# A token-mixing layer on one core: the fifth tile of x gets a load of its own

## Chip, core and metric

The kernel runs on one core of a Trainium2 chip. The metric is the time of one execution on the device in microseconds, and the median over several executions is compared. In the text, PE is the tensor engine, ACT the scalar engine, DVE the vector engine, POOL the general-purpose engine, and SP the engine that only issues transfers here.

## What is computed

The input `x` has 2048 tokens of 640 features in bf16. A linear attention with 32 heads of 20 features and a gated MLP mixer both work on it, and a gate of one number per token mixes the two.

```python
def _A_ref(x, wqkv, wo):
    qkv = (x @ wqkv).reshape(B, S, 3, H, Dh)        # S 2048, H 32, Dh 20; then per head
    phi = lambda t: jnp.where(t > 0, t + 1, jnp.exp(t)) + 1e-6
    pq, pk = phi(q), phi(k)
    kv = jnp.einsum("bhsd,bhse->bhde", pk, v)
    z = jnp.einsum("bhsd->bhd", pk)
    num = jnp.einsum("bhqd,bhde->bhqe", pq, kv)
    den = jnp.einsum("bhqd,bhd->bhq", pq, z)[..., None] + 1e-6
    return concat_heads(num / den) @ wo

def _B_ref(x, w1, w2, w3, w4):
    h = _gelu(_layernorm(x) @ w1)
    hs = shift_quarters(h) @ w2                     # quarters of h moved by 1, -1, 2, -2 tokens
    x1 = x + hs
    return x1 + _gelu(_layernorm(x1) @ w3) @ w4

g = _sigmoid((x * gate_w).sum(-1, keepdims=True))
return g * _A_ref(...) + (1 - g) * _B_ref(...)
```

## The kernel before

The tokens are cut into 16 tiles of 128. Each tile is held once as it comes (`x_tok`, tokens on the partitions) and once turned (`xT`, features on the partitions), because the projections need the features on the partitions. For each tile t the kernel computes q (`q_tile`, L864) and k (`k_tile`, L781): five matmuls of 512 columns and five of 128 or 130 each, then `phi` (L772): an Exp on ACT, and two operations on DVE that leave the result in bf16. In the text, q4 is the q matmuls of tile 4, k3 the k matmuls of tile 3, and so on.

The order in which PE does this is written out by hand at the start and planned afterwards. It begins with warm-up matmuls; tiles 0 to 2 are turned by PE itself; then q of tiles 0 to 2 (`q_three`), k of tiles 0 and 1 (`k_two`), k2, and from tile 3 on q and k in turn, q3, k3, q4, k4. From k4 on a short matmul for the gram matrix of x and k (`gt_tail`, L798) stands after each pair. After tile 15 come the rest of that gram matrix, the mixer's `w1` and `w2`, then `w3`, the attention output and `w4`.

A planner (`_Items`) models how long each step takes and picks the next one, and the tracker `_Sched` adds the semaphore waits that the data require. Each engine runs its own list of instructions in order.

Tiles 3 to 15 are turned by the DMA engines. `x_turn(t)` (L692) issues one transposing transfer on SP; it has to wait until the tile has landed in `x_tok`. SP's list at the start, in order, is:

1. the loads of tile 0, tile 1, the first 128-row slice of wq, tile 2, and the four other slices of wq
2. the first slice of the k weights (`wkg`), the load of tile 3, and the four other slices of `wkg`, the last at L688
3. the turn of tile 3 (L695), which waits for the load of tile 3
4. a load of tiles 4 to 7 in one transfer of 640 KB (L700), then the four turns of these tiles (L702)
5. the same for tiles 8 to 11 and for tiles 12 to 15

Every load above except those in 4 and 5 has 160 KB. As SP's list is in order, the load of tiles 4 to 7 is issued once the turn of tile 3 has been issued, and the load of tiles 8 to 11 once the turn of tile 7 has been issued.

POOL issues loads too, on a queue of its own, when certain k tiles are done: `load_w1` (L706) after k5, `load_w2` (L714) after k8, and `wv` and `wo` after k11. These share the 16 DMA engines with the turns of the later tiles.

Of the kernel before, what the change touches and what calls it, by code (L numbers as in the profile page):

```python
# [416 lines left out]
def _build(nc, A_x, A_wqkv, A_wo, B_w1, B_w2, B_w3, B_w4, gate_w, out, dbg=None, stop=None):  # L417
# [61 lines left out]
    x_tok = pa.alloc("x_tok", [128, NT, D], BF16)  # L479
# [191 lines left out]
    x2 = A_x[0]  # L671

    def dma_in(out_ap, in_ap, key, **kw):
        return sch.dma("sp", out_ap, in_ap, key, **kw)
# [17 lines left out]
    def x_turn(t):  # L692
        sch.dma("sp", xT[:, :, 128 * t:128 * (t + 1)], x_tok[:, t, :], "trx%d" % (t % 4), transpose=True)

    x_turn(3)  # L695
    gwr = xn[:, 1, 0:128]
    dve(lambda e: e.memset(gwr, 0.0), [], [gwr])
    sch.dma("act", xn[0:KD, 1, 0:128], gate_w.rearrange("(k p) -> k p", p=128), "gw")
    for c in range(1, NCH):
        dma_in(x_tok[:, 4 * c:4 * c + 4, :], x2[512 * c:512 * (c + 1), :].rearrange("(n p) d -> p n d", p=128), "xc%d" % c)  # L700
        for t in range(4 * c, 4 * c + 4):
            x_turn(t)  # L702

# [499 lines left out]
    for t in range(NT):  # L1203
        c = t // 4
# [53 lines left out]
    for t in range(NT):  # L1258
        c = t // 4
# [30 lines left out]
def bass_gated_mix__linear_attn_block__mixer_s_mlp__prompt_kernel(  # L1290
    nc, A_x, A_wqkv, A_wo, B_x, B_w1, B_w2, B_w3, B_w4, gate_w, out
):
    assert tuple(A_x.shape) == (1, S, D) and tuple(out.shape) == (1, S, D)
    assert tuple(A_wqkv.shape) == (D, 3 * D) and tuple(A_wo.shape) == (D, D)
    assert tuple(B_w1.shape) == (D, D) and tuple(B_w2.shape) == (D, D)
    assert tuple(B_w3.shape) == (D, F) and tuple(B_w4.shape) == (F, D) and tuple(gate_w.shape) == (D,)
    _build(nc, A_x, A_wqkv, A_wo, B_w1, B_w2, B_w3, B_w4, gate_w, out)
# [28 lines left out]
```

## Time and profile before

| what | us |
|---|---|
| median of 5 executions | 260.59 |
| the five | 260.57, 260.58, 260.59, 262.31, 262.43 |
| the profiled execution | 260.59 |
| its span in the trace | 259.3 |
| outside the span | 1.29 |
| PE busy in the span | 255.6 |
| granted PE clock, mean | 1.00 of full speed |

The span runs from the first to the last instruction in the trace. Matmuls are pipelined, and their ends are modelled: where two groups follow one another without a gap, the modelled end of the first lies after the start of the second. How long PE really stood is therefore read from the starts.

The three 640 KB loads of x, from issue to landing, took 4.4, 4.3 and 6.7 us. The 160 KB loads of x took 2.4 to 3.7 us, and the five of the k weights 3.8 to 4.0 us. The thirteen turns took between 2.4 and 8.7 us to land, 2.8 in the median, and each costs SP about 1.28 us to issue.

### The profile page before, as it was taken

Reading aid. Unit: us, or ns where it says so; the run is one execution under the profiler, and the core shown is the slowest. Engines: PE = TensorE matmul, PEld = TensorE weight load, DVE = VectorE, ACT = ScalarE, POOL = GpSimd, SP = SyncE. Lnnn points to the kernel's source line nnn. Section 1 sums busy time; section 2 is a strip of 40 time slices with the busy share of each in tenths; the row PEclk is TensorE's granted clock in tenths of the full one; section 3 lists DMA queues with packets and bytes.
Section 4 is the critical chain, followed back from the end, with each engine's and each line's share of the span. In section 5 each row is a group of like instructions: output and inputs, shape, how many; then the busy total and the mean of one; then the engine's idle time right before and its main releaser. Section 6 shows DMA issues by size and latency. Waiting matters only on the chain.

```text
span 259.3 us, 4291 instructions
## 1 busy us (share of the span) xinstructions
PE 255.6 (99%) x1685; PEld 131.9 (51%) x1685; DVE 152.6 (59%) x288; ACT 106.7 (41%) x216; POOL 93.7 (36%) x151
## 2 busy tenths in 40 slices
PE   7999999999999999999999999999999999999996
PEld 4555555544454554555444545554455644456453
DVE  2587887899913799999998407992033410143233
ACT  1496677751355766675854240005500045200000
POOL 4013995969954019667904202230011110021001
PEclk9999999999999999999999999999999999999999
DMA  6855989982856992552826650232000020000211
GB/s 183 237 139 151 131 222 158 201 133 50 99 110 125 346 344 42 67 101 52 104 47 122 124 74 0 44 87 73 0 3 0 3 101 0 0 3 1 104 51 51
DMA packets 51390, 25.16 MB, mean 97 GB/s; under 512 B 42750, under 2 KB 49959, under 8 KB 51370
## 3 DMA queue, kind: packets, MB, share of 16 engines
q1 hardware_dynamic: 49984, 21.47, 38.1%
q0 software_dynamic: 1136, 3.28, 5.4%
q8 instruction: 13, 0.21, 0.4%
q10 hardware_dynamic: 250, 0.14, 0.2%
q14 instruction: 7, 0.06, 0.1%
HBM read 12.05 MB, written 2.62 MB: 57 GB/s over the span
## 4 chain that ended last, share of the span: by engine, by line
PE 92%; DMA 4%; SPq 2%; DVE 0%; issue 0%
PE ps L600 60%; PE ps L1165 22%; PE ps L794 8%; DMA x_tok<-in_A_x_dram 3%; SPq L285 1%; DMA xT<-x_tok 1%; PE ps L1077 1%; PE ps L1147 1%; SPq L281 1%; DVE x_tok L639 0%; PE ps L967 0%; PE ps L996 0%; PE ps L1144 0%
## 5 line engine op out<-in xcount | busy, mean ns | idle before, releaser
L600 PE MATMUL ps<-xnT,w 128*128 128x512 bf16 x360 | 81.5, 379 | 0.0
L1165 PE MATMUL ps<-w,h2T 128*128 128x512 bf16 (+1 forms) x416 | 58.8, 299 | 0.0
L656 ACT ACTIVATE h2T<-ps 128x512 bf16<-128x512 f32 x52 | 30.5, 598 | 67.5 <-PE ps L600 67.5
L600 PEld LDWEIGHTS ps<-xnT,w 128*128 128x128 bf16 x360 | 34.2, 98 | 38.5 <-issue 0.9
L639 DVE SCALAR_TENSOR_TENSOR x_tok<-ps,stg,abx 128x512 bf16<-128x512 f32 (+1 forms) x32 | 17.3, 550 | 61.5 <-PE ps L1165 61.5
L622 POOL TENSOR_SCALAR abx<-x_tok,stg 128x640 f32<-128x640 bf16 x16 | 15.3, 959 | 98.9 <-DVE x_tok L639 94.9
L1165 PEld LDWEIGHTS ps<-w,h2T 128*128 128x128 bf16 x416 | 32.2, 98 | 24.9 <-issue 1.1
L622 POOL TENSOR_SCALAR xn<-x_tok,st 128x640 bf16<-128x640 bf16 x32 | 34.9, 1099 | 14.5 <-DMA xnT<-xn 13.9
L656 ACT ACTIVATE Er<-ps 128x640 bf16<-128x640 f32 x32 | 22.4, 707 | 17.1 <-PE ps L600 8.7
L655 ACT ACTIVATE junk<-x_tok 128x640 bf16<-128x640 bf16 x32 | 23.6, 739 | 3.1 <-DVE x_tok L637 2.6
L600 PE MATMUL ps<-M_sb,pqnT 128*128 128x512 bf16 (+1 forms) x160 | 24.3, 299 | 0.0
L656 ACT ACTIVATE hsT<-ps 128x512 bf16<-128x512 f32 (+1 forms) x32 | 18.9, 593 | 13.0 <-PE ps L600 12.7
L600 PE MATMUL ps<-w,hsT 128*128 128x512 bf16 (+1 forms) x160 | 23.7, 299 | 0.0
L639 DVE SCALAR_TENSOR_TENSOR abx<-ps,stg,abx 128x640 f32<-128x640 f32 x16 | 14.1, 884 | 12.4 <-PE ps L600 11.4
L600 PE MATMUL ps<-wkg,xT 128*128 128x130 bf16 (+1 forms) x140 | 21.4, 299 | 0.0
L600 PE MATMUL ps<-wq,xT 128*128 128x512 bf16 (+1 forms) x130 | 19.8, 299 | 0.2 <-DMA xT<-x_tok 0.2
L600 PEld LDWEIGHTS ps<-w,hsT 128*128 128x128 bf16 x160 | 13.3, 98 | 12.1
L600 PEld LDWEIGHTS ps<-M_sb,pqnT 128*128 128x128 bf16 x160 | 13.2, 98 | 10.9
L794 PE MATMUL ps<-pk_tok,x_tok 128*128 128x512 bf16 x80 | 17.8, 379 | 0.0
L622 DVE TENSOR_SCALAR Er<-Er 128x640 bf16<-128x640 bf16 x32 | 11.8, 369 | 9.7 <-ACT Er L656 9.6
L1106 DVE TENSOR_TENSOR pq_tok<-pq_tok,dnr 128x300 bf16<-128x300 bf16 (+1 forms) x48 | 16.9, 407 | 0.6
L637 DVE SCALAR_TENSOR_TENSOR x_tok<-ps,x_tok 128x640 bf16<-128x640 f32 x16 | 13.1, 821 | 6.4 <-PE ps L600 5.9
(78 smaller groups left out, 227.0 us busy)
## 6 DMA issues: line engine op xcount, KB each, us to landing
w<-in_B_w_dram SPq DMA_DIRECT2D x1, 2160.0 KB, 9.9
w<-in_B_w_dram SPq DMA_DIRECT2D x1, 2080.0 KB, 15.5
x_tok<-in_A_x_dram SPq DMA_DIRECT2D x3, 640.0 KB, 4.4
out_dram<-x_tok SPq DMA_DIRECT2D x3, 640.0 KB, 3.1
w<-in_B_w_dram POOLq DMA_DIRECT2D x8, 160.0 KB, 5.2
wq<-in_A_wqkv_dram SPq DMA_DIRECT2D x5, 160.0 KB, 3.9
wkg<-in_A_wqkv_dram SPq DMA_DIRECT2D x5, 160.0 KB, 3.9
wv<-in_A_wqkv_dram POOLq DMA_DIRECT2D x1, 800.0 KB, 5.6
```

The costliest lines, as they stand in the source:

```text
L281: return e.dma_start_transpose(out_ap, in_ap)
L285: return e.dma_start(out_ap, in_ap)
L600: ins = e.matmul(out_ap, l, r, start=(i == 0), stop=(i == n - 1))
L622: return engf(lambda e: e.tensor_scalar(out_ap, in_ap, s1, s2, op0, op1), rd, [out_ap], cost=cost)
L637: return dve(lambda e: e.scalar_tensor_tensor(out_ap, in0, scalar, in1, op0, op1, accum_out=accum), rd, [out_ap, accum], cost=cost + 70.0)
L639: return dve(lambda e: e.scalar_tensor_tensor(out_ap, in0, scalar, in1, op0, op1), rd, [out_ap], cost=cost)
L655: return act(lambda e: e.activation(out_ap, in_ap, func, bias=bias, scale=scale, accum_out=accum), rd, wr, cost=cost)
L656: return act(lambda e: e.activation(out_ap, in_ap, func, bias=bias, scale=scale), rd, wr, cost=cost)
L794: ins = e.matmul(o, l, r, start=(t0 + q_ == 0), stop=(t0 + q_ == NT - 1))
L1077: ins = e.matmul(o, l, r, start=st, stop=sp)
L1106: dve(lambda e, o=o, i0=i0, i1=i1: e.tensor_tensor(o, i0, i1, ALU.mult), [i0, dnr[:, 1, sd, :]], [o], cost=cost)
L1165: ins = e.matmul(o, l, r, start=False, stop=(i == KFF - 1), skip_group_check=(n0 > 0))
```

## The change

Tile 4 gets a load of its own. It is issued right behind the last slice of the k weights and ahead of the turn of tile 3. The next transfer then brings tiles 5 to 7 only, three tiles with 480 KB instead of four, and is issued where the load of tiles 4 to 7 was. The turn of tile 4 follows it as before, but waits for its own load and not for the transfer of tiles 5 to 7. The first turn that waits for that transfer is that of tile 5.

```diff
     def x_turn(t):
         sch.dma("sp", xT[:, :, 128 * t:128 * (t + 1)], x_tok[:, t, :], "trx%d" % (t % 4), transpose=True)
 
+    dma_in(x_tok[:, 4, :], x2[512:640, :], "x4")
     x_turn(3)
     gwr = xn[:, 1, 0:128]
...
     for c in range(1, NCH):
-        dma_in(x_tok[:, 4 * c:4 * c + 4, :], x2[512 * c:512 * (c + 1), :].rearrange("(n p) d -> p n d", p=128), "xc%d" % c)
+        t0 = 5 if c == 1 else 4 * c
+        dma_in(x_tok[:, t0:4 * c + 4, :], x2[128 * t0:512 * (c + 1), :].rearrange("(n p) d -> p n d", p=128), "xc%d" % c)
         for t in range(4 * c, 4 * c + 4):
             x_turn(t)
```

SP issues one transfer more. The order of the instructions on PE, DVE, ACT and POOL, and the places of their buffers, are the same in both kernels. One instruction on DVE no longer waits for ACT, and one on ACT also waits for an earlier one of ACT; both belong to the mixer's `w2` stage.

## The prediction

> **What bounds the kernel now.** I read the page's busy shares and its chain shares first, then the chain in order of time, the waits of the tensor engine, its timeline around the one wait it has on a load, and last the landings of the transfers that share the queue.
>
> ```profile
> PE 255.6 (99%) x1685; PEld 131.9 (51%) x1685; DVE 152.6 (59%) x288; ACT 106.7 (41%) x216; POOL 93.7 (36%) x151
> PE 92%; DMA 4%; SPq 2%; DVE 0%; issue 0%
> ```
>
> PE (columns: busy us, share, instructions) is the bound. Only what shortens PE's work or fills a hole in it moves the end. The change issues the same matmuls, so the holes count.
>
> ```profile
> 5.03 3.75 DMA x_tok<-in_A_x_dram
> 8.79 1.31 SPq L281
> 10.10 0.05 issue
> 10.15 4.41 DMA x_tok<-in_A_x_dram
> 14.58 2.42 DMA xT<-x_tok
> 17.00 0.05 issue
> 17.05 2.89 PE ps L600 x20
> ```
>
> This is the chain of waits (start us, length, what). Up to 17.05 us it runs through SP's queue: x tile 3 lands at 8.79, its turn is issued for 1.31, then the 640 KB load of tiles 4-7 takes 4.41, and tile 4's turn 2.42. From 17.05 to the last eviction the chain is PE alone, without a hole: a shift at 17.05 should arrive at the end.
>
> ```profile
> PE ps L860 <- PEq L1311: 0.8, 1, 0.8
> PE ps L887 <- DMA wq<-in_A_wqkv_dram: 0.5, 1, 0.5
> PE ps L600 <- DMA xT<-x_tok: 0.2, 1, 0.2
> PEld ps L600 <- DMA xT<-x_tok: 0.4, 1, 0.4
> ```
>
> All of PE's waits (total us, times, longest), and the weight load's wait on a turn. The change touches only the xT one. 0.2 is counted from the modelled end of the last matmul; the true size is in the starts:
>
> ```profile
> 12.56 1.52 PE L600 MATMUL ps<-wkg,xT 128*128 128x512 bf16 x10
> 13.92 1.52 PE L600 MATMUL ps<-wq,xT 128*128 128x512 bf16 x10
> 15.28 1.52 PE L600 MATMUL ps<-wkg,xT 128*128 128x512 bf16 x10
> 17.05 1.53 PE L600 MATMUL ps<-wq,xT 128*128 128x512 bf16 x10 [0.24 <-DMA xT<-x_tok]
> ```
>
> k2, q3 and k3 start 1.36 us apart; q4 would follow at 15.28 + 1.36 = 16.64 or 16.65 and starts at 17.05. The hole is 0.40 us.
>
> **What the Trainium skill says.** "TensorE: Matmul & The Clock Gate", section "Back-to-back issue gap", gives N/2.4 + 2.5 ns between warm matmuls: five of 512 and five of 128 columns are an estimated 1.36 us, as the trace has it, so the 0.40 is idle array and nothing else is in it. "DMA: Bandwidth & Descriptors", section "Queues, rings and completion order", says that on each DMA engine a queue's descriptors are consumed in ring order and that different queues take turns by packets. The trace bears out both: x3 lands 3.75 us after its issue where x1, with an emptier queue, took 2.4; and turns that take 2.4 to 2.5 us alone take up to 8.7 beside POOL's loads.
>
> **The change, part by part.**
> *Added: one 160 KB load of tile 4.* SP's last wkg issue ends at 5.50 + 1.85 = 7.35, then SP stood until 8.79 for x3. The new issue (0.43, as the other 160 KB ones) fills 7.40 to 7.83: nothing. Without that cover it would delay turn 3's issue by 0.43. The wkg slices in front of it took 3.8 to 4.0 us to land, so I take tile 4's landing at 7.40 + 4.0 = 11.4; 2.4 us in an empty queue (9.8) is the lower end, 5 us (12.4) the upper. The wq and wkg loads stand ahead of it in the queue and aren't touched.
> *Turn 3, now behind 160 KB more.* The queue moves about 330 GB/s there (windows 7 to 9 us), 164 kB are 0.5 us, so turn 3 lands at 11.6 + 0.35 to 0.5 = 12.1 at most. q3 needs it at 13.92: nothing, with 1.8 to spare.
> *The slice of tiles 5-7.* Still issued at 10.15 (0.57), 480 instead of 640 KB: at 370 GB/s (window 13 to 14 us) 164 kB less are 0.44, so it lands near 14.1; 14.58 is the bound.
> *Turn 4, with a new wait on its own load.* SP is free at 10.72 and waits to 11.4. Behind it stand turns 5-7 and later loads; turn 5 can't go before 14.1, so nobody feels the wait. Issued at 11.4, its packets could start 1.2 us later (the DMA view by windows, before: issued 14.58, packets from 15.75), but they stand behind the 480 KB in the same queue, drained at about 13.6 (14.05 before, less 0.44). Packets 0.67, landing 0.6 after the last (as before): 14.9. Lower end 13.9; upper end, were it held until the slice has landed and then took its full 2.42, 14.58 + 2.42 = 17.0, which is no gain. PE is ready at 16.65, so my value has 1.7 us to spare.
> *Turns 5-7 and what follows.* Turn 5 goes at 14.1 instead of 15.85; three turns of 1.28 end at 18.0 instead of 19.74. The loads of tiles 8-11 and 12-15 and their turns go some 1.8 us earlier. q5 needs its turn at 20.2; it lands at 16.5.
> *What is late next at 16.65?* By the DVE timeline and the order in which PSUM pairs go round, the pair that q4 takes (k1's) was released at 15.50, k4's (k2's) at 16.88 against 18.0, the gram tail's at 18.25 against 19.4, k5's at 20.55 against 21.55. ACT is behind here (busy without a break from 12.21 to 18.40), so q4's Exp starts at 18.40 instead of 18.62, and the 0.66 us breaks that follow take the rest. No PE wait is made.
> *Order.* PE, POOL, banks and buffers are as before; one DVE and one ACT instruction of a later stage trade a wait, both in stages where these engines idle. Nothing.
> Sum: -0.40 us. The profiled execution is 260.59 (span 259.3 and 1.29 around it) and equals the median of the five runs shown: 260.59 - 0.40 = 260.2.
>
> **The rivals.**
> *A. No gain: turn 4 lands as late as before.* It stands behind the slice in one queue, so it isn't freed of it. For it: ring order. Against it: it must come 1.7 us later than worked out. Time 260.4 to 260.6.
> *B. Slower: the gap goes to turn 14.* Turns 12-15 run beside POOL's w1 and w2 loads:
>
> ```profile
> 38.63 2.84 SPq L281 DMA_TRANSPOSE xT<-x_tok  x2
> xT<-x_tok SPq DMA_TRANSPOSE x1, 8.7
> 47.48 1.40 PEld L600 LDWEIGHTS ps<-wq,xT 128*128 128x128 bf16 x10
> ```
>
> Turn 14 is issued at 38.63 and lands 8.7 us later, at 47.33 (the second line is that turn's issue row: time to landing); q14's weights load at 47.48. That is a margin of 0.15 us. PE now comes at 47.08, while SP's issues move 1.8 earlier and POOL's only 0.4, so these streams meet differently. If turn 14's landing stays tied to the end of POOL's packets, 0.25 of the gain is lost (260.45). From a landing after 47.5 on, each further microsecond is a microsecond of PE. That such sizes occur is seen in the five runs: three at 260.57 to 260.59 and two at 262.31 and 262.43, and the trace, of a 260.59 execution, doesn't show where those 1.75 us lie. Were they there and met in the median run, it gives 260.2 + 1.75 = 261.95. Against it: turns 12-14 issued earlier get ahead of w2's packets, which begin at 37.4; turn 14 would go near 37. I expect the margin to grow. But if the 1.75 has another cause, it can still fall in the median run: same time.
> *C. Faster by more than the hole.* PE's other holes in the trace are the first 0.83, 0.5 on wq and 0.17 on a bank, and the change touches none. Below 259.3 I see no mechanism; a small chance for what one trace can't show.
>
> **How the numbers follow.** Forecast 0.64 (own range 259.9 to 260.4), A with the small loss in B 0.12 (to 260.8), B at about 262.0 with 0.19, C 0.05. What a measurement can tell from no change is about 0.5%, 1.3 us: below 259.3 is faster, above 261.9 slower. The forecast and A are both "same": 0.76. These two alone leave more than 2 in 10 out, so the range goes from 259.8 to 262.1; the likeliest case alone is 259.9 to 260.4.
>
> **What would show it.** Right: the tile 4 load issued near 7.4; turn 4 landed before 16.6; no PE wait on xT near 17; q4 at 16.65; the last PE work 0.4 earlier. Wrong: a PE wait on xT still at q4 (A), one at q12 to q15 (B), or a wait on a bank or on wkg between 10 and 24 us, which my spare times exclude.

## The result and the profile after

| | before | after |
|---|---|---|
| median, us | 260.87 (80 executions) | 260.51 (43) |
| fastest, us | 260.43 | 259.91 |
| slowest, us | 262.60 | 261.70 |
| above 261.5 us | 15 of 80 | 1 of 43 |
| the profiled execution, us | 260.59 | 261.04 |
| its span, us | 259.3 | 259.8 |

The ratio of after to before is 0.9978, with a 95% interval of 0.9971 to 0.9986. It is the ratio of the means, 260.52 and 261.08: the change saves about 0.57 us (0.22%) in the mean. The medians, which the prediction spoke of, differ by 0.36 us; 0.40 was predicted. The larger sample moved the median of the kernel before from 260.59 to 260.87, so the median after is 260.51 and not the predicted 260.2. Two things changed: the fastest execution is 0.5 us faster, and the executions above 261.5 us have nearly gone.

The profile after begins with its shares and its chain of waits (start us, length, what).

```profile
PE 256.6 (99%) x1685; PEld 132.5 (51%) x1685; DVE 152.2 (59%) x288; ACT 106.6 (41%) x216; POOL 93.8 (36%) x151
PE 97%; DMA 1%; DVE 1%; SPq 0%; issue 0%
```

```profile
13.60 6.80 PE ps L600 x50
```

The chain before went through SP's queue up to 17.05 us. Here it is PE that stands in the chain at 13.60, and 50 matmuls follow one another: k2, q3, k3, q4 and k4. The DMA and SP shares of the chain fall from 4% and 2% to 1% and 0%. All that is left of PE's waits is outside the change:

```profile
PE ps L862 <- PEq L1313: 0.8, 1, 0.8
PE ps L889 <- DMA wq<-in_A_wqkv_dram: 0.2, 1, 0.2
```

The timeline of PE around q4 (start us, length, what) shows the hole closed:

```profile
14.80 1.52 PE L600 MATMUL ps<-wq,xT 128*128 128x512 bf16 x10
16.16 1.53 PE L600 MATMUL ps<-wkg,xT 128*128 128x512 bf16 x10
17.52 1.52 PE L600 MATMUL ps<-wq,xT 128*128 128x512 bf16 x10
```

q4 follows k3 after 1.36 us, where it was 1.77 before. Lines of SP's own timeline and the issue row of tile 4's turn (last figure: us to landing) say why:

```profile
7.40 0.43 SPq L285 DMA_DIRECT2D x_tok<-in_A_x_dram  x1
10.24 0.57 SPq L285 DMA_DIRECT2D x_tok<-in_A_x_dram  x1
11.61 6.99 SPq L281 DMA_TRANSPOSE xT<-x_tok  x4
18.64 0.58 SPq L285 DMA_DIRECT2D x_tok<-in_A_x_dram  x1
28.31 0.94 SPq L285 DMA_DIRECT2D x_tok<-in_A_x_dram  x1
35.07 5.16 SPq L281 DMA_TRANSPOSE xT<-x_tok  x4
```

```profile
xT<-x_tok SPq DMA_TRANSPOSE x1, 3.3
```

Tile 4's turn is issued at 11.61 and lands 3.3 us later, at 14.9, 2.6 us ahead of q4. The later loads of x go out at 18.64 and 28.31 instead of 19.78 and 29.32, and the last four turns begin at 35.07 instead of 36.05. What that does to tile 12 is seen in the issue row of its turn and in the start of q12 on PE, first in the profile of before, then in that of after:

```profile
xT<-x_tok SPq DMA_TRANSPOSE x1, 4.8
41.54 1.52 PE L600 MATMUL ps<-wq,xT 128*128 128x512 bf16 x10
```

```profile
xT<-x_tok SPq DMA_TRANSPOSE x1, 2.4
42.01 1.52 PE L600 MATMUL ps<-wq,xT 128*128 128x512 bf16 x10
```

Before, the turn lands at 36.05 + 4.8 = 40.8, 0.7 us ahead of q12; after, at 35.07 + 2.4 = 37.5, 4.5 us ahead. In the same way the turns of tiles 13 to 15 landed 2.7, 0.2 and 2.4 us ahead of their q before, and 5 to 6 us ahead after.

The profiled execution is longer than that of before, although the kernel is faster. The reason lies in the first 7 us of PE (two of its matmuls of 512 columns):

```profile
6.09 0.63 PE L889 MATMUL ps<-wq,xT 128*128 128x512 bf16 x1
6.94 0.38 PE L889 MATMUL ps<-wq,xT 128*128 128x512 bf16 x1
```

The first of these two equal matmuls still runs at the slow rate, the second at the full one. In the profile of before the full rate was there from 4.09 us on. So q3 starts at 14.80 here and at 13.92 there, 0.88 us later. From q4 to the end of the span both take the same: 259.3 - 17.05 = 242.25 and 259.8 - 17.52 = 242.28. Of the fourteen profiles of this case thirteen show 242.2 to 242.4 there, so an execution's time is the start of q4 and a constant; the one exception is the late wait of experiment 4. Without the 0.88 us this execution would be 260.16.

### The profile page after: what moved, and what is told of

Its sections match the earlier page's. It is cut to its first block, busy times and chain, and to the rows that moved or that the text cites. A ratio compares the mean times of both kernels' runs of the same rounds, so it can differ in the third digit from the quotient of the medians.

```text
span 259.8 us, 4292 instructions
## 1 busy us (share of the span) xinstructions
PE 256.6 (99%) x1685; PEld 132.5 (51%) x1685; DVE 152.2 (59%) x288; ACT 106.6 (41%) x216; POOL 93.8 (36%) x151
## 4 chain that ended last, share of the span: by engine, by line
PE 97%; DMA 1%; DVE 1%; SPq 0%; issue 0%
PE ps L600 61%; PE ps L1167 22%; PE ps L796 8%; PE ps L889 2%; DMA wq<-in_A_wqkv_dram 1%; PE ps L1079 1%; PE ps L1149 1%; PE ps L890 1%; DVE x_tok L639 0%; PE ps L969 0%; PE ps L998 0%; SPq L285 0%; DVE xT L665 0%; PE ps L1146 0%; PE ps L611 0%
## 5 line engine op out<-in xcount | busy, mean ns | idle before, releaser
L639 DVE SCALAR_TENSOR_TENSOR abx<-ps,stg,abx 128x640 f32<-128x640 f32 x16 | 14.1, 884 | 12.4 <-PE ps L600 11.3
L600 PEld LDWEIGHTS ps<-w,hsT 128*128 128x128 bf16 x160 | 13.3, 98 | 12.1
```

What stands on the lines that cost most here:

```text
L600: ins = e.matmul(out_ap, l, r, start=(i == 0), stop=(i == n - 1))
L639: return dve(lambda e: e.scalar_tensor_tensor(out_ap, in0, scalar, in1, op0, op1), rd, [out_ap], cost=cost)
```

## The experiments

Two theories were set against each other. **H**: all of the gain is tile 4's turn, whose lateness before varies between executions. **L**: a good part of it lies at the last turns, 12 to 15, which go out about 1 us earlier and so meet POOL's w2 load differently; the long executions of the kernel before are then waits on these turns.

**1. The early tile 4 without the early late turns.** A second turn of tile 6 (extra work, same data) behind tile 7 pushes SP's later issues back.

```diff
         for t in range(4 * c, 4 * c + 4):
             x_turn(t)
+        if c == 1:
+            x_turn(6)
```

> The changed kernel with tile 6 turned a second time behind tile 7 (extra work, same data), so that the load of tiles 8-11 and all that follows on SP go some 1.3 us later, near their places before the change; turn 4 keeps its early load. Theory L (a good part of the gain is that turns 12-15 get ahead of POOL's w2 load): executions above 261.0 us come back (39% of the executions before, 2% after), median 260.6 to 260.9, ratio to before 0.998 to 1.000. Theory H (all of the gain is turn 4, whose lateness varies from 0.4 to 2 us before): as the changed kernel, median 260.5, ratio about 0.998, next to none above 261.0.

Measured: ratio 1.0000, interval 0.9984 to 1.0015; median 260.90; fastest 260.10; 11 of 22 above 261.0 and 7 of 22 above 261.5, six of these between 262.00 and 262.54 and one, which the ratio leaves out, at 264.42. Turn 12 was issued at 36.29, near its 36.05 of before. The fastest executions keep the gain and the long ones are back. Its profile, of an execution at 260.37, has no hole at q4 but shows a small one at q13 (starts on PE):

```profile
41.22 1.52 PE L600 MATMUL ps<-wq,xT 128*128 128x512 bf16 x10
42.58 1.53 PE L600 MATMUL ps<-wkg,xT 128*128 128x512 bf16 x10
43.94 0.43 PE L798 MATMUL ps<-x_tok,pk_tok 128*128 128x512 bf16 x2
44.33 1.53 PE L600 MATMUL ps<-wq,xT 128*128 128x512 bf16 x10
```

q13 comes 3.11 us after q12 instead of 2.99: 0.12 us of waiting for a turn even in this short execution (tile 13's turn took 6.8 us and landed at 44.3). H fails as an account of the whole gain.

**2. The kernel before with w2 out of the way.** Tile 4 stays as it was; the eight w2 transfers go on SP behind the turn of tile 15.

```diff
         for t in range(4 * c, 4 * c + 4):
             x_turn(t)
+    for g_ in range(4):
+        dma_in(w2[:, g_, :], B_w2[160 * g_:160 * g_ + 128, :], "w2", group_total=8)
+        dma_in(w2[32 * g_:32 * (g_ + 1), 4, :], B_w2[160 * g_ + 128:160 * (g_ + 1), :], "w2", group_total=8)
...
     def load_w2():
-        dp = [k_done[8]]
...
+        return
```

> The kernel before, with the eight w2 transfers issued on SP behind the turn of tile 15 and not on POOL beside the turns of tiles 12-15. Turn 4 is as before, so the hole at q4 stays. Theory L: the executions above 261.0 us vanish, the fastest stays near 260.4, median 260.6 to 260.7, ratio to before 0.998 to 0.999. Theory H: the spread is that of the kernel before, median 260.9, ratio 1.000.

Measured: ratio 0.9979, interval 0.9966 to 0.9993; median 260.77 against 261.03 in the same session; fastest 260.42, as before; none of 22 above 261.5, where the kernel before had 11 of 43. Seven still lie between 261.0 and 261.41, more than L had named. Over all executions of the session the means, 260.85 and 261.19, differ by 0.34 us, less than the ratio says and within its interval. The issue row of turn 12 in its profile, issued at 35.67:

```profile
xT<-x_tok SPq DMA_TRANSPOSE x1, 2.9
```

With w2 away it lands 2.9 us after its issue, where it took 4.8 before. The head of this kernel up to q4 is that of the kernel before, so what went with w2 was not a slow head.

**3. Both: the place of experiment 1, with w2 on SP as in 2.**

> The run with tile 6 turned twice (late turns back at their old places, turn 4 early), now with the w2 transfers on SP behind turn 15 as in the second run. Theory L: its slow executions (half above 261.0 us, up to 264.4) came from the meeting with w2 and vanish; median 260.5, at most one in ten above 261.0, ratio to before 0.997 to 0.998, like the changed kernel. Rival: the second turn itself or the late place costs the time whatever POOL loads; then a third or more stay above 261.0 and the ratio is 0.999 to 1.001.

Measured: ratio 0.9983, interval 0.9972 to 0.9994; fastest 260.15; one of 22 above 261.0 (261.04). The long executions of experiment 1 were its meeting with w2, not its extra turn. The median, 260.72, is higher than expected. The profile shows one reason that may be part of it: tile 4's turn took 5.4 us from its issue at 11.52, landed near 16.95, and q4 came 0.20 us late.

**4. Looking for a long execution of the kernel before.** Four more profiles of the unchanged kernel were taken. For the first two, two theories and a third case were put down:

> The kernel before once more, for a second profile. If this execution is above 261 us: theory L expects PE to wait for xT at one of q12 to q15 (40 to 51 us) and for at most 0.4 us at q4; theory H expects the wait at q4, 17 us, longer than 1 us; a third case is a later start of q0 with neither. If it is near 260.6: turn 14 lands within 0.5 us of q14's weight load.

> The kernel before a third time, for another profile; the same readings as in the second. With 39% of the executions above 261 us, at least one of the two should lie there with a chance of about 0.6.

They came out at 260.89 and 261.08. The second lay above 261 and had neither of the waits that L and H expected, and turn 14 landed 0.1 us before q14 in the first and 2.1 us in the second. In both, the full rate of the array came later than in the first profile (q3 at 14.45 and 14.68), and the hole at q4 was 0.18 and 0.12 us instead of 0.41. Still it was tile 4's turn that set q4: it landed at 17.31 and 17.48 instead of 17.00, q4 began 0.04 us later each time, and the times are longer by these 0.3 and 0.5 us. That much of H holds. Two more followed:

> The kernel before once more, for a profile of an execution above 261.4 us (a quarter of them). Theory L: PE waits for xT at one of q12 to q15 for 0.5 to 2 us. Theory H: the wait is at q4. If it lies below 261.1 it repeats the two readings already there: no PE wait on xT above 0.4 us.

> As the run before it: a further profile of the kernel before, with the same readings.

The last was another of the same kind (261.03, hole 0.20, turn 4 landed at 17.45). The one before it ran 261.31 us, a little under what it was meant to catch, and shows the wait that L expected. PE's timeline:

```profile
38.55 1.52 PE L600 MATMUL ps<-wq,xT 128*128 128x512 bf16 x10
39.91 1.52 PE L600 MATMUL ps<-wkg,xT 128*128 128x512 bf16 x10
41.27 0.43 PE L794 MATMUL ps<-x_tok,pk_tok 128*128 128x512 bf16 x2
42.27 1.53 PE L600 MATMUL ps<-wq,xT 128*128 128x512 bf16 x10 [0.56 <-DMA xT<-x_tok]
```

and SP's, with the issue rows (last figure: us to landing) of the load of tiles 12 to 15 and of tile 12's turn:

```profile
29.30 0.58 SPq L285 DMA_DIRECT2D x_tok<-in_A_x_dram  x1
37.08 5.39 SPq L281 DMA_TRANSPOSE xT<-x_tok  x4
```

```profile
x_tok<-in_A_x_dram SPq DMA_DIRECT2D x1, 640.0 KB, 7.8
xT<-x_tok SPq DMA_TRANSPOSE x1, 5.1
```

q12 would follow q11 after 2.99 us, at 41.54; it starts at 42.27, 0.73 us late. Tile 12's turn was issued at 37.08 and landed at 42.2. Two delays add up: the 640 KB load, issued at 29.30 beside POOL's w1, took 7.8 us instead of 6.7, and the turn, beside w2, took 5.1 us. The rest of this profile is like the first, the hole of 0.4 at q4 included: 260.59 + 0.73 = 261.32, and 261.31 was measured.

**5. Trying for more: the first wq slice ahead of tiles 1 and 2.** With the hole closed, the start of q0 bounds the head.

```diff
     dma_in(x_tok[:, 0, :], x2[0:128, :], "x0")
-    dma_in(x_tok[:, 1, :], x2[128:256, :], "x1")
...
     load_wq(0)
+    dma_in(x_tok[:, 1, :], x2[128:256, :], "x1")
     dma_in(x_tok[:, 2, :], x2[256:384, :], "x2")
```

> The changed kernel with the first wq slice issued before the loads of tiles 1 and 2, so that it lands some 0.45 us earlier. With the hole at q4 filled, the start of q0 is what bounds the first 20 us: q0 begins near 4.6 instead of 5.0 to 5.4 us and the whole shifts, median 260.1 to 260.3. Rival: tile 1, now 0.45 us later, holds the turn by PE in front of q0, or the array's cold clock sets the head; then 260.4 to 260.6 as the changed kernel.

Measured: median 262.04, ratio 1.0020, interval 0.9999 to 1.0041. The times fall apart: six between 260.53 and 260.95, eight between 262.02 and 262.80. The short ones already refute the expected gain: in the profile PE waits 0.7 us for tile 1 before it turns it, and q0 starts at 5.38. Profiles were then taken to find the long ones:

> The kernel with the first wq slice issued first, once more, for a profile of one of its executions near 262.5 us (8 of 14 lay above 262.0, 6 below 261.0). Theory C (the 0.7 us that PE now stands in front of the turn of tile 1 leaves the array slow for longer): the 128x512 matmuls of q0 to q2 start 0.43 us apart instead of 0.22 until 8 us or later, q3 starts near 16 instead of 14.4, and PE has no wait on xT above 0.5 us from q4 on. Theory L (late turns): the head is as in the profile at 260.61, and a wait of 1 to 2 us stands at one of q12 to q15.

The first ran 260.40 us, and a second (same expectation) 260.81. A third caught a long one:

> The kernel with the first wq slice issued first, a last time, since both profiles before this one fell near 260.6. If it lies above 262: theory C expects q3 near 16 us and half-speed starts in q0 to q2 beyond 8 us, theory L a wait of 1 to 2 us at one of q12 to q15. If it lies below 261, the split of this kernel's times stays open.

It ran 262.50 us. Its matmuls of 512 columns on PE near 8 us, and below them those of the execution at 260.40:

```profile
8.26 0.63 PE L889 MATMUL ps<-wq,xT 128*128 128x512 bf16 x1
8.79 0.63 PE L889 MATMUL ps<-wq,xT 128*128 128x512 bf16 x1
9.33 0.47 PE L889 MATMUL ps<-wq,xT 128*128 128x512 bf16 x1
```

```profile
7.88 0.38 PE L889 MATMUL ps<-wq,xT 128*128 128x512 bf16 x1
8.15 0.38 PE L889 MATMUL ps<-wq,xT 128*128 128x512 bf16 x1
```

From one such matmul to the next it takes 0.53 us in the first and 0.27 in the second: the array is at half rate until about 9.4 us. q3 starts at 16.25 instead of 14.16, and 2.09 us is the difference of the two times (262.50 - 260.40 = 2.10). No wait on a turn stands anywhere. This is theory C's picture, and it says that the late waits of L are not the only source of long executions. That the hole in front of tile 1 brings the late switch is a guess: it was not tried by itself, and the three short executions that were profiled have nearly the same hole (0.57 to 0.75 us, against 0.76 in the long one). The eight long executions of the list above have no profile of their own.

**6. The changed kernel with w2 on SP as well.**

> The changed kernel with the w2 transfers on SP behind turn 15 as well. Theory L: the changed kernel has taken turns 12 to 15 out of w2's way already, so this adds nothing: median 260.4 to 260.6, at most one in ten above 261.0, ratio to before 0.997 to 0.9985. Rival (w2 still costs something there, or SP's longer list delays the turns of the normalized tiles): a median away from 260.5 by more than 0.2.

Measured: ratio 0.9979, interval 0.9968 to 0.9989; median 260.57; 260.05 to 261.00, none above 261.0. It is the changed kernel's time. There the turns of tiles 13 to 15 still run beside w2, but with 5 to 6 us to spare, so taking w2 away gains nothing. No version here beats the changed kernel clearly.

Executions above 261.5 us, leaving out experiment 5 with its other cause: before 40 of 185, after 1 of 43; turn 4 early and late turns in their old place 7 of 22; w2 away in three kernels 0 of 66. So it is shown that w2 beside the turns makes the long executions. No execution of the kernel before near 262.5 was caught in a profile. That it is the same kind of wait, only longer, is argued from these counts and not seen.

## Why the prediction held, point by point

- **The bound and the arithmetic of the shift.** From q4 to the end both traces take 242.25 and 242.28 us: what is gained at q4 arrives at the end, as said. Taking out the 0.88 us of slow array, the profiled execution is 260.16; 260.2 was predicted.
- **Tile 4's load and turn.** The load went out at 7.40. The turn was issued at 11.61 (11.4 predicted), landed at 14.9 (14.9 predicted), and PE had no wait. That the landing was met so exactly is partly luck: in the three profiles of other kernels with the same head it was 15.7 (experiment 1), near 16.35 (experiment 6, 0.2 us ahead of q4) and near 16.95 (experiment 3, q4 late by 0.20), close to the upper end of 17.0. The 1.7 us to spare are not there in every execution, and rival A is in part true in some.
- **Turn 3 and the slice.** Turn 3 landed at 12.3, a little past the 12.1 put as its most, and far from the 14.80 where q3 wanted it. The slice landed at 14.1 as predicted. Turn 5 landed at 17.9 and not at 16.5, still in time for q5.
- **SP's later issues.** 1.8 us earlier was predicted; 1.14 was measured at the load of tiles 8 to 11 and 1.0 at the turn of tile 12. The term that failed is the sum of three turns at 1.28 us each: the four turns with the wait took 6.99 us, since the issue of tile 6's turn took 1.87; why is not shown.
- **The size, 0.40 us.** In the median the change is worth 0.36 us, near the 0.40, but the sum was another one: two of its terms were off in opposite directions, and that they nearly cancel is luck. The hole at q4 was read from one execution. In five profiles of the kernel before it is 0.41, 0.18, 0.12, 0.42 and 0.20, 0.27 in the mean, because a slow array in the first 7 us makes PE late for tile 4, and the hole then takes up what the array lost. The fastest executions differ by 0.3 to 0.5 us (260.43 before; 259.91 after, and 260.05 to 260.15 in the other kernels with the same early tile 4). The rest, about 0.3 of the 0.57 us in the mean, is the second gain at the late turns, which the sum put at nothing; taking w2 away by itself gave 0.34 in experiment 2.
- **Rival B.** It had the right place to look, the turns beside POOL's loads with their small margin, and the 1.75 us in the five first times as a sign of it. It drew the wrong side: the margin was what the kernel before lost, and the earlier issues gave it back. The text expected the margin to grow, and turn 14 landed at 42.8 instead of 47.3, but counted no gain for it. The waits that were seen are at q12, whose turn depends on the 640 KB load, and at q13 in experiment 1, and not at q14. But turn 14 landed only 0.1 to 0.2 us ahead of q14 in two of the five profiles of before, so it may be late too in those that were not caught.

## What to carry to other kernels

One profile shows one execution. Where a wait has a margin of a few tenths beside a shared queue, as turn 12 had with 0.7 us, it is a cost in some executions and none in others, so a list of many times says more than another look at the same trace. An edit that moves a whole in-order queue earlier should be credited at each later wait, not only at the one it was made for: here about half of the gain in the mean came at the turns of tiles 12 to 15, some 25 us and more after q4. And a hole on the bounding engine is worth its full size only while that engine isn't late by itself.

## What the hardware showed that was not expected

The array's rate in the first microseconds differs between executions of one kernel. In the first profile of the kernel before, full rate was reached before 4.1 us, in three other profiles of it between 6 and 6.5; in that of after it came near 6.5, and near 9.4 in the long execution of experiment 5, which cost 2.1 us. The granted clock was 1.00 in each of these profiles and doesn't show it; the lengths of equal matmuls do (0.63 and 0.38 us). The Trainium skill, "TensorE: Matmul & The Clock Gate", section "What's actually happening", describes a window of about 3.4 us that runs freely; after a busy one the rate doubles. The times here are compatible with that: a window missed at half rate would cost half of it, an estimated 1.7 us from that page's figure, and the medians of the two groups of experiment 5 (260.63 and 262.54) lie 1.9 us apart. That a window was missed is not shown.

The turns' time to land depends on what other queues move: 2.4 to 2.9 us for turn 12 with w2 away, 3.6 to 5.1 beside it, and up to 8.9 for turn 14.
